# Second-stage attention scores: one float32 matmul replaced by three float32r passes over split q and k

## The chip, the cores and the metric

The kernel runs on one core of one Trainium2 chip. Its time is the device time of one execution in microseconds; the time before is the median of three runs. A separate, profiled execution gives the trace from which all durations below are read. PE is TensorE's matmul row, PEld its weight loads, DVE is VectorE, ACT is ScalarE, POOL is GpSimd, SP issues the DMAs.

## The reference

Two layers follow each other, with 8 batches of 576 tokens.

```python
# layer 1: 8 heads of width 64; heads 0-3 see the last 32 tokens, heads 4-7 every 32nd earlier token
scores = scale * np.matmul(q, k.transpose(0, 1, 3, 2))
scores = np.where(masks[None], scores, -1e9)
attn = softmax(scores);  x = np.matmul(attn, v)          # x: (8, 576, 512) after the heads are joined
# layer 2: 4 experts, each a causal attention of width 64 over x; the top 2 of 4 gate logits weigh them
logits = x @ w_gate
for e in range(4):
    q = x @ wq[e];  k = x @ wk[e];  v = x @ wv[e]
    scores = scale * (q @ k.transpose(0, 2, 1))
    scores = np.where(causal, -1e9, scores)
    a = softmax(scores)
    out += weight_of_e * (a @ v @ wo[e])
```

`wq` and `wk` are drawn eight times larger than the other weights, so the second layer's scores are wide and have to be computed with nearly full float32 precision.

## The kernel before, in words

Layer 1 is done per batch and pair of heads: `load_qk` brings q and k into a tile `nat`, `tp` (L514) transposes it on PE, `s` (L546) makes scores, `mask` and `softmax0` to `softmax5` run on DVE, POOL and ACT, `pt` (L604, L607) transposes the weights back, `xa` (L641, L658) multiplies with v. The result x is held as two float32r tiles, `xh` (rounded) and `xl` (the remainder).

Layer 2 is done per batch b and pair of experts ep (two pairs, so 16 rounds in all). `project` (L765, for the first batch L776) makes q and k of both experts of a pair at once: 128 rows, 64 for each expert, in two column halves of 288 tokens. Each half is twelve passes of 128 rows by 288 columns, three for each of the four slices of x (`xh` with the rounded weight, `xl` with the rounded weight, `xh` with the weight's remainder). `pj_out` copies each half from PSUM into the float32 tile `qk`, on ACT or DVE. `values2` (`vp`, L712) makes v and the gate logits the same way.

`attend` makes the scores. The 576 queries are four tiles of 128 and one of 64; tile t sees 128, 256, 384, 512 and 576 keys. For a 128-query tile (`s2`, L839) the two experts lie in rows 0 to 63 and 64 to 127 and are two float32 matmuls, each into a PSUM bank of its own. The last 64 queries (`s2_4`, L819) of both experts share one bank, expert 0 in partitions 0 to 63 and expert 1 in 64 to 127, in two key halves of 288. Then come `max2` and `max2_4` (DVE, L846, L825: scale, mask, row maximum), `exp2` (ACT, L851), `recip2` (DVE), `scale2` (POOL, L874), `t2` (L893, transposes on PE), `acc` (L926, times v), a split into `oh` and `ol`, and `yp` (L955, the output projection), whose result is stored.

PE knows four array shapes here: 128x128 (`pj`, `vp`, `yp`), row-split 64x128 (`tp`, `pt`, `s2`, `t2`), column-split 128x64 (`acc`, local `xa`) and 64x64 (`s`, `s2_4`, the other `xa`).

The order on each engine is written at build time. Every operation is registered with `op(kind, engines, key, ...)`, with an assumed duration for each engine that may take it, the buffers it reads and writes, and a key that is shifted by the table `PRI` (per kind, and per kind and batch). `schedule()` (L214) then walks through time and lets each engine take, among the operations that could start now, the one with the lowest key; buffers come from rings (`Ring`) of fixed size. What comes out is a fixed instruction stream for each engine: on the chip each engine runs its own in order, and a late operand holds up everything behind it. The rings that the change touches are `QK2` (the `qk` tiles, three), `TH` (transposed weights, four) and `PTR` (transposed layer-1 weights, two). While the kernel starts, the raw weights wq, wk and wv stand in the three `QK2` tiles, from where `hi_w` and `lo_w` split them.

Of the kernel before, what the change touches and what calls it, by code (L numbers as in the profile page):

```python
# [9 lines left out]
F32R = mybir.dt.float32r  # L10
# [10 lines left out]
def attention_moe_kernel(  # L21
# [59 lines left out]
    class Ring:  # L81
# [26 lines left out]
        "acc": 14.5, "acc 0": -193.0, "acc 1": 158.0, "acc 2": 1.0, "acc 3": 17.0, "acc 5": 37.5,  # L108
# [13 lines left out]
        "lo_w 0": -52.5, "load_qk": -6.0, "load_qk 0": -264.5, "load_qk 1": -15.0, "load_qk 2": -24.5,  # L122
        "load_qk 3": 76.0, "load_qk 4": 68.0, "load_qk 5": 107.5, "load_qk 6": 127.0, "load_qk 7": 164.0,
        "load_v": 6.0, "load_v 0": 5.5, "load_v 1": 5.5, "load_v 2": 30.0, "load_v 3": 36.0,
        "load_v 4": 15.5, "load_v 5": 55.5, "load_v 6": 96.5, "load_v 7": 74.5, "load_w": 9.0,
        "load_w 0": 21.0, "mask": 21.0, "mask 0": 137.5, "mask 1": -30.0, "mask 2": 124.0, "mask 3": 19.0,
# [248 lines left out]


    YS = ring("ys", [128, DM], 3)
    QK2 = ring("qk2", [128, 2, S], 3)
    W = {}

    def load_weights(name, key):
# [6 lines left out]
        for kt in range(nk):  # L388
# [3 lines left out]
            def raw(kt=kt, st=st):  # L392
                if wide:
                    return wide.t.rearrange("p a c -> p (a c)")[:, kt * n:kt * n + n]
# [636 lines left out]
```

## Time and profile before

| what | value |
|---|---|
| time, median of 3 runs | 492.1 us (491.94 to 493.04) |
| the profiled execution's own time | 494.44 us |
| its span, first to last instruction | 492.7 us |
| mean granted TensorE clock | 0.982 |
| PE busy | 473.5 us, 96% |
| DVE, ACT, POOL busy | 323.8, 293.8, 201.5 us |

Busy time of PE counts every matmul from its start to its modelled end, and these overlap; what a matmul costs the stream behind it is read from the distance between two starts in the timeline. A float32 matmul stands in the trace as two records (128 `s2` matmuls of the program are 256 records of L839), a float32r matmul as one. A group's tile name has its buffer number left out, and operands are given as partitions x columns.

### The profile page before, as it was taken

Reading aid. Unit: us, or ns where it says so; the run is one execution under the profiler, and the core shown is the slowest. Engines: PE = TensorE matmul, PEld = TensorE weight load, DVE = VectorE, ACT = ScalarE, POOL = GpSimd, SP = SyncE. Lnnn points to the kernel's source line nnn. Section 1 sums busy time; section 2 is a strip of 40 time slices with the busy share of each in tenths; the row PEclk is TensorE's granted clock in tenths of the full one; section 3 lists DMA queues with packets and bytes.
Section 4 is the critical chain, followed back from the end, with each engine's and each line's share of the span. In section 5 each row is a group of like instructions: output and inputs, shape, how many; then the busy total and the mean of one; then the engine's idle time right before and its main releaser. Section 6 shows DMA issues by size and latency. Waiting matters only on the chain.

```text
span 492.7 us, 17597 instructions
## 1 busy us (share of the span) xinstructions
PE 473.5 (96%) x7046; PEld 398.0 (81%) x7046; DVE 323.8 (66%) x1004; ACT 293.8 (60%) x838; POOL 201.5 (41%) x252
## 2 busy tenths in 40 slices
PE   7679999899999999999999999899999999999996
PEld 5569897789778888898778987688978897898774
DVE  5777778784689467775878646675577857616620
ACT  2557867564765368655786536565486647635642
POOL 5456655532365143451473424133236434501430
PEclk9877999999999999999999999999999999999999
DMA  7988942530156004730466101454043100200024
GB/s 144 175 156 185 172 109 70 115 73 25 36 167 171 1 2 115 183 65 2 100 178 165 56 0 48 142 130 87 25 108 120 38 0 24 93 25 1 1 85 129
DMA packets 88880, 43.35 MB, mean 88 GB/s; under 512 B 77024, under 2 KB 80480, under 8 KB 88800
## 3 DMA queue, kind: packets, MB, share of 16 engines
q1 hardware_dynamic: 88800, 42.24, 35.4%
q8 instruction: 56, 0.92, 0.8%
q14 instruction: 24, 0.20, 0.1%
HBM read 32.78 MB, written 9.44 MB: 86 GB/s over the span
## 4 chain that ended last, share of the span: by engine, by line
PE 90%; DMA 6%; SPq 2%; issue 1%; ACT 0%; ACTq 0%
PE bank L765 19%; PE bank L712 12%; PE bank L955 11%; PE bank L926 9%; PE bank L839 8%; PE bank L893 6%; DMA nat<-in_k_dram 6%; PE bank L514 5%; PE bank L546 4%; PE bank L641 4%; PE bank L819 4%; PE bank L776 3%; PE bank L658 3%; PE bank L604 2%; PE bank L607 1%; SPq L460 1%
## 5 line engine op out<-in xcount | busy, mean ns | idle before, releaser
L874 POOL TENSOR_SCALAR p<-p,st,wt 128x256 f32<-128x256 f32 (+3 forms) x128 | 75.8, 607 | 110.1 <-DVE st L858 44.7
L851 ACT ACTIVATE p<-p,st 128x128 f32<-128x128 f32 (+3 forms) x128 | 71.3, 560 | 10.8 <-DVE st L846 10.8
L846 DVE CUSTOM_DVE_ANT_0 p<-bank,m_cau 128x128 f32<-128x128 f32 (+3 forms) x128 | 56.6, 486 | 19.1 <-PE bank L839 17.2
L329 ACT COPY qk<-bank 128x288 f32<-128x288 f32 x48 | 19.2, 400 | 53.7 <-PE bank L765 50.4
L926 PE MATMUL bank<-th,vs 128*64 128x192 f32 (+4 forms) x512 | 50.5, 343 | 0.0
L329 ACT COPY th<-bank 128x256 f32<-128x256 f32 (+2 forms) x100 | 40.2, 428 | 13.0 <-PE bank L893 11.5
L329 ACT COPY qkt<-bank 128x324 f32<-128x324 f32 (+2 forms) x99 | 36.6, 424 | 18.4 <-PE bank L514 14.4
L572 POOL TENSOR_TENSOR p1l<-p1l,st 128x960 f32<-128x960 f32 (+1 forms) x18 | 29.1, 1626 | 42.7 <-DVE st L570 31.0
L926 PEld LDWEIGHTS bank<-th,vs 128*64 128x64 f32 x512 | 34.7, 138 | 14.1 <-issue 7.2
L712 PE MATMUL bank<-wh_v,xh 128*128 128x260 f32 (+1 forms) x160 | 46.0, 288 | 0.0
L712 PE MATMUL bank<-wh_v,xl 128*128 128x260 f32 (+1 forms) x160 | 45.3, 283 | 0.0
L712 PE MATMUL bank<-wl_v,xh 128*128 128x260 f32 (+1 forms) x160 | 45.2, 282 | 0.0
L893 PEld LDWEIGHTS bank<-ident,p 64*128 64x128 f32 x800 | 32.3, 139 | 15.3 <-issue 9.7
L839 PE MATMUL bank<-qk 64*128 64x128 f32 (+3 forms) x256 | 42.1, 449 | 0.0
L329 DVE COPY th<-bank 128x384 f32<-128x384 f32 (+2 forms) x60 | 29.1, 489 | 19.6 <-PE bank L893 17.4
L893 PE MATMUL bank<-ident,p 64*128 64x64 f32 x800 | 40.7, 230 | 0.0
L581 POOL TENSOR_TENSOR p1l<-p1l,st 128x960 f32<-128x960 f32 (+1 forms) x18 | 29.0, 1616 | 27.8 <-DVE st L579 24.3
L514 PE MATMUL bank<-ident,nat 54*128 54x54 f32 (+1 forms) x636 | 30.8, 233 | 8.5 <-DMA nat<-in_k_dram 7.2
L546 PE MATMUL bank<-qkt 64*64 64x54 f32 (+1 forms) x1408 | 35.0, 239 | 3.7 <-ACT qkt L329 1.6
L514 PEld LDWEIGHTS bank<-ident,nat 54*128 54x128 f32 (+1 forms) x636 | 25.8, 146 | 12.8 <-issue 7.5
L546 PEld LDWEIGHTS bank<-qkt 64*64 64x64 f32 x1408 | 29.8, 138 | 6.6 <-ACT qkt L329 3.2
L765 PE MATMUL bank<-xh,wh_k 128*128 128x288 f32 x112 | 33.8, 302 | 0.0
(138 smaller groups left out, 1241.3 us busy)
## 6 DMA issues: line engine op xcount, KB each, us to landing
out_dram<-ys SPq DMA_DIRECT2D x32, 256.0 KB
v<-in_v_dram SPq DMA_DIRECT2D x32, 192.0 KB
nat<-in_q_dram SPq DMA_DIRECT2D x28, 144.0 KB
nat<-in_k_dram SPq DMA_DIRECT2D x28, 144.0 KB
nat<-in_q_dram SPq DMA_DIRECT2D x32, 99.0 KB
nat<-in_k_dram SPq DMA_DIRECT2D x32, 99.0 KB
v<-in_v_dram SPq DMA_DIRECT2D x48, 54.0 KB
nat<-in_q_dram SPq DMA_DIRECT2D x16, 90.0 KB
```

Source lines behind the costliest of these rows:

```text
L329: (nc.scalar.copy if e == "ACT" else nc.vector.tensor_copy)(dst, src)
L514: nc.tensor.transpose(tp[x].t[:, w_ * (g - g0):w_ * (g - g0) + w_], blk, ident[r, r])
L546: nc.tensor.matmul(o, lhs, rhs, start=True, stop=True)
L712: nc.tensor.matmul(vp.t[:m, :NV], xx.t[:, t0:t0 + m], ww.t[:, kt, :], start=i == 0, stop=i == 11)
L765: nc.tensor.matmul(pj.t[:, :HS], ww.t[:, kt, ep * 128:(ep + 1) * 128], xx.t[:, c], start=i == 0, stop=i == 11)
L839: nc.tensor.matmul(sp[a].t[:, :nk], qk.t[r, 0, q0:q0 + 128], qk.t[r, 1, :nk], start=True, stop=True)
L846: lambda e, sp=sp, p=p, a=a, nk=nk, ci=ci: nc.vector.tensor_tensor_reduce(out=p.t[:, a, :nk], in0=sp[a].t[:, :nk], in1=m_cau[:, S - nk:], ...
L851: op("exp2", {"ACT": 0.485 + 0.00083 * nk}, k_ + 1, lambda e, p=p, a=a, ci=ci, nk=nk: nc.scalar.activation(p.t[:, a, :nk], p.t[:, a, :nk], ...
L874: lambda e, p=p, a=a, ci=ci, t=t, nk=nk: nc.gpsimd.tensor_scalar(p.t[:, a, :nk], p.t[:, a, :nk], st.t[:, 14 + ci + a:15 + ci + a], wt.t[:, ...
L893: nc.tensor.transpose(tp[hf].t[:, 64 * c:64 * c + 64], src, ident[r, r])
L926: nc.tensor.matmul(acc.t[o, c0:c0 + cn], vw, th[a].t[:, s0:s0 + cn], start=j == 0, stop=j == idx[-1], skip_group_check=True)
L955: nc.tensor.matmul(yp.t[:, :DM], xx.t[:, c0:c0 + 128], ww.t[:, ep, :], start=i == 0, stop=i == 5)
```

## The change

1. `pj_out` now always runs on ACT and writes `qk` rounded to float32r. A new operation `pj_lo` (DVE) subtracts this from the projection in PSUM and writes the remainder to a new tile `qkl` (float32r).
2. `s2` (L864 in the new file) is three float32r passes for each expert, accumulated in the same bank: q with k, q's remainder with k, q with k's remainder. The two experts' passes alternate.
3. For the last 64 queries a new operation `qd` (POOL, four copies of 64x64) lays q and its remainder of both experts on the diagonal of a 128x128 tile whose other half is zero. `s2_4` (L844) is then three full 128x128 passes of 288 columns instead of two float32 matmuls, and its array shape is that of the projections.
4. Buffers: `QK2` has two tiles instead of three, two `qkl` and two `qd` tiles are new, `PTR` has one instead of two. The raw weights wq and wk are staged in the `TH` tiles, wv in the tiles `P2[2]` of the weights of score tile 2.
5. Every entry of `PRI` has another value, and there are entries for `pj_lo` and `qd`.

```diff
     PRI = {
-        "acc": 14.5, "acc 0": -193.0, "acc 1": 158.0, "acc 2": 1.0, "acc 3": 17.0, "acc 5": 37.5,
+        "acc": 22.0, "acc 0": -338.0, "acc 1": 87.0, "acc 2": 51.5, "acc 3": 110.5, "acc 4": 29.0,
...
-    QK2 = ring("qk2", [128, 2, S], 3)
+    QK2 = ring("qk2", [128, 2, S], 2, F32R)
+    QKL = ring("qkl", [128, 2, S], 2, F32R)
+    QD = fixed("qd", [128, 2, 128], 2, F32R)
+    for t in QD.tiles:
+        for a in range(2):
+            nc.scalar.copy(t[64 * a:64 * a + 64, :, 64 - 64 * a:128 - 64 * a],
+                           m_cau[64 * a:64 * a + 64, :128].rearrange("p (i c) -> p i c", i=2))
...
-        wide = QK2.new(f"wst_{name}") if name != "o" else None
+        wide = [] if name == "o" else [(P2[2] if name == "v" else TH).new(f"wst_{name}{i}") for i in range(2)]
...
-    PTR = ring("pt1", [128, 2 * 2 * 5 * 64], 2)
+    PTR = ring("pt1", [128, 2 * 2 * 5 * 64], 1)
...
-            op("pj_out", either(HS), key + step * u + 0.5, lambda e, u=u, pj=pj: copy(
-                e, qk.t[:, j, u * HS:(u + 1) * HS], pj.t[:, :HS]), r=[pj], w=[qk[j, u]])
+            c_ = slice(u * HS, (u + 1) * HS)
+            op("pj_out", {"ACT": act(HS)}, key + step * u + 0.5, lambda e, c_=c_, pj=pj: nc.scalar.copy(
+                qk.t[:, j, c_], pj.t[:, :HS]), r=[pj], w=[qk[j, u]])
+            op("pj_lo", {"DVE": dve(HS)}, key + step * u + 0.8, lambda e, c_=c_, pj=pj: nc.vector.tensor_sub(
+                qk.lo.t[:, j, c_], pj.t[:, :HS], f(qk.t[:, j, c_])), r=[pj, qk[j, u]], w=[qk.lo[j, u]])
+        if j == 0:
+
+            def diag(e):
+                for i, x in enumerate((qk, qk.lo)):
+                    for a in range(2):
+                        r = slice(64 * a, 64 * a + 64)
+                        nc.gpsimd.tensor_copy(qk.d.t[r, i, r], f(x.t[r, 0, S - 64:]))
+
+            op("qd", {"POOL": 1.2}, key + step + 1, diag, r=[qk[0, 1], qk.lo[0, 1]], w=[qk.d])
...
-                        for a in range(2):
-                            r = slice(64 * a, 64 * a + 64)
-                            nc.tensor.matmul(sp.t[r, :HS], qk.t[r, 0, q0:q0 + 64], qk.t[r, 1, c0:c0 + HS],
-                                             start=True, stop=True)
+                        for i, (l, r) in enumerate(((0, qk), (1, qk), (0, qk.lo))):
+                            nc.tensor.matmul(sp.t[:, :HS], qk.d.t[:, l], r.t[:, 1, c0:c0 + HS], start=i == 0, stop=i == 2)
...
-                for a in range(2):
-                    r = slice(64 * a, 64 * a + 64)
-                    nc.tensor.matmul(sp[a].t[:, :nk], qk.t[r, 0, q0:q0 + 128], qk.t[r, 1, :nk], start=True, stop=True)
+                for i, (x, y) in enumerate(((qk, qk), (qk.lo, qk), (qk, qk.lo))):
+                    for a in range(2):
+                        r = slice(64 * a, 64 * a + 64)
+                        nc.tensor.matmul(sp[a].t[:, :nk], x.t[r, 0, q0:q0 + 128], y.t[r, 1, :nk], start=i == 0, stop=i == 2)
```

How this moves instructions is read from the built streams. First PE at the scores of the third batch, second pair of experts. Before, the last projection passes (L765) are followed by the four tiles of `s2` (L839), one matmul per expert and tile:

```order
L765 MATMUL bank6_70<-xl1_180,wh_q0_221 128x288
L765 MATMUL bank6_70<-xh1_174,wl_q0_222 128x288
L839 MATMUL bank1_65<-qk22_136 128x128
L839 MATMUL bank2_66<-qk22_136 128x128
L839 MATMUL bank4_68<-qk22_136 128x256
L839 MATMUL bank5_69<-qk22_136 128x256
L839 MATMUL bank7_71<-qk22_136 128x384
L839 MATMUL bank0_64<-qk22_136 128x384
L839 MATMUL bank3_67<-qk22_136 128x512
L839 MATMUL bank6_70<-qk22_136 128x512
```

The same place now (`qk2` is the rounded q and k, `qkl` the remainder; L779 is the projection, L864 the scores):

```order
L779 MATMUL bank2_66<-xl1_190,wh_q0_227 128x288
L779 MATMUL bank2_66<-xh1_184,wl_q0_228 128x288
L864 MATMUL bank4_68<-qk21_135 128x128
L864 MATMUL bank7_71<-qk21_135 128x128
L864 MATMUL bank4_68<-qk21_135,qkl1_137 128x128
L864 MATMUL bank7_71<-qk21_135,qkl1_137 128x128
L864 MATMUL bank4_68<-qkl1_137,qk21_135 128x128
L864 MATMUL bank7_71<-qkl1_137,qk21_135 128x128
L864 MATMUL bank1_65<-qk21_135 128x256
L864 MATMUL bank0_64<-qk21_135 128x256
```

A tile has three matmuls per expert where it had one, and the two experts' banks alternate. Here the twelve passes that fill bank2_66 (the last half of q) stand between the half that the first two tiles need and the first score pass. Counted over the whole PE stream, the array shape changes 259 times where it changed 249 times.

Second, ACT and DVE around the projections of the second batch's first pair of experts, in the new streams. On ACT, L799 is `pj_out`:

```order
L334 COPY ys0_131<-bank6_70 128x512
L799 CAST qk20_134<-bank2_66 128x288
L799 CAST qk20_134<-bank4_68 128x288
L334 COPY vs1_197<-bank3_67 128x260
L589 ACTIVATE p1s0_172<-p1s0_172 128x12x54
```

On DVE, L801 is `pj_lo`, L574 and L585 belong to layer 1's softmax:

```order
L574 TENSOR_TENSOR p1s1_175<-bank1_65,m_str_81 128x6x54
L801 TENSOR_TENSOR qkl0_136<-bank2_66,qk20_134 128x288
L585 TENSOR_REDUCE st12_181<-p1s0_172 128x12
L585 TENSOR_REDUCE st13_182<-p1s1_175 128x12
L801 TENSOR_TENSOR qkl0_136<-bank4_68,qk20_134 128x288
```

All 64 copies of projected q and k stand on ACT now (48 stood there and 16 on DVE), and DVE has 64 subtractions more, each behind its copy and in line with layer 1's reductions. Third, POOL for the same pair of experts, where L809 is `qd`, L596 the last softmax step of layer 1 and L899 is `scale2`:

```order
L596 TENSOR_TENSOR p1s1_175<-p1s1_175,st13_182 128x12x54
L809 CAST qd0_138<-qk20_134 64x64 x2
L809 CAST qd0_138<-qkl0_136 64x64 x2
L899 TENSOR_SCALAR p200_144<-p200_144,st24_209,wt1_204 128x128 x2
```

The four copies are new on POOL (64 in the whole program). The last-queries matmuls (`s2_4`) stand on PE as three passes in each of the two key halves. On SP the loads while the kernel starts stand in nearly the same order: half of wk has moved from behind the loads of the second batch's third pair of heads (L467 before, L482 now) to ahead of them.

More of the change, by code (lines that the diff above doesn't have):

```diff
@@ L107, in attention_moe_kernel @@
     PRI = {
-        "acc": 14.5, "acc 0": -193.0, "acc 1": 158.0, "acc 2": 1.0, "acc 3": 17.0, "acc 5": 37.5,
[13 rows of a table removed]
[L122 to L126, printed above, removed]
[54 rows of a table removed]
+        "acc": 22.0, "acc 0": -338.0, "acc 1": 87.0, "acc 2": 51.5, "acc 3": 110.5, "acc 4": 29.0,
[13 rows of a table added]
+        "hi_w 0": -109.0, "lo_w": -136.0, "lo_w 0": -81.0, "load_qk": -71.5, "load_qk 0": -231.5,
+        "load_qk 1": 42.5, "load_qk 2": 62.5, "load_qk 3": 62.5, "load_qk 4": 48.5, "load_qk 5": 53.0,
+        "load_qk 6": 118.5, "load_qk 7": 126.5, "load_v": 64.0, "load_v 0": -64.5, "load_v 1": -53.5,
+        "load_v 2": -5.5, "load_v 3": 12.5, "load_v 4": 103.5, "load_v 5": 85.5, "load_v 6": 60.5,
+        "load_v 7": 56.0, "load_w": 1.0, "load_w 0": 12.5, "mask": -142.0, "mask 0": 196.5, "mask 1": -43.0,
[10 rows of a table added]
+        "pj_lo 6": -117.5, "pj_lo 7": 197.0, "pj_out": -189.5, "pj_out 0": -8.5, "pj_out 1": 326.5,
[38 rows of a table added]
+        "vp_out": -284.5, "vp_out 0": 186.0, "vp_out 1": 209.0, "vp_out 2": -203.0, "vp_out 3": 60.5,
+        "vp_out 4": 242.0, "vp_out 5": 1.0, "vp_out 6": 18.0, "vp_out 7": 18.5, "warm": 148.5,
[6 rows of a table added]
+        "yp_out": -38.0, "yp_out 0": -354.0, "yp_out 1": 56.5, "yp_out 2": 74.5, "yp_out 3": 88.5,
+        "yp_out 4": -22.5, "yp_out 5": 103.5, "yp_out 6": -149.0, "yp_out 7": 44.0,
     }
@@ L377, in attention_moe_kernel @@
     YS = ring("ys", [128, DM], 3)
-    QK2 = ring("qk2", [128, 2, S], 3)
+    QK2 = ring("qk2", [128, 2, S], 2, F32R)
[5 more added lines that the diff above has]
+                           m_cau[64 * a:64 * a + 64, :128].rearrange("p (i c) -> p i c", i=2))
     W = {}
+    P2 = [ring(f"p2{t}", [128, 2, S if t == 3 else q0 + m], 2) for t, (q0, m) in enumerate(QT[:4])]
+    P2.append(fixed("p24", [128, S + 64], 2, value=lambda t: [t[:, S:]]))
+    TH = ring("th", [128, 832], 4)
     def load_weights(name, key):
@@ L386, in load_weights @@
         W[name] = (hi, lo)
-        wide = QK2.new(f"wst_{name}") if name != "o" else None
+        wide = [] if name == "o" else [(P2[2] if name == "v" else TH).new(f"wst_{name}{i}") for i in range(2)]
         for kt in range(nk):
-            st = wide[kt] if wide else YS.new(f"wst_{name}{kt}")
+            st = wide[kt // 2][kt % 2] if wide else YS.new(f"wst_{name}{kt}")
             k_ = key + 0.1 * kt
@@ L393, in raw @@
                 if wide:
-                    return wide.t.rearrange("p a c -> p (a c)")[:, kt * n:kt * n + n]
+                    t = wide[kt // 2].t
+                    t = t.rearrange("p a c -> p (a c)") if name == "v" else t
+                    return t[:, kt % 2 * n:kt % 2 * n + n]
                 return st.t
@@ L414, in load_weights @@
                r=[st, hi[kt]], w=[lo[kt]])
-    P2 = [ring(f"p2{t}", [128, 2, S if t == 3 else q0 + m], 2) for t, (q0, m) in enumerate(QT[:4])]
-    P2.append(fixed("p24", [128, S + 64], 2, value=lambda t: [t[:, S:]]))
     NAT = fixed("nat", [128, (11 * 2 + 1) * D], 2, value=lambda t: [t[:, c * D:(c + 1) * D] for c in (10, 21, 22)])
@@ L683, in attention_moe_kernel @@
     ST2 = ring("st2", [128, 24], 6)
-    TH = ring("th", [128, 832], 4)
     OHR = ring("oh", [128, DM], 3, F32R)
@@ L816, in mml @@
                     def mml(e, sp=sp, c0=c0, q0=q0):
-                        for a in range(2):
-                            r = slice(64 * a, 64 * a + 64)
-                            nc.tensor.matmul(sp.t[r, :HS], qk.t[r, 0, q0:q0 + 64], qk.t[r, 1, c0:c0 + HS],
-                                             start=True, stop=True)
-                    op("s2_4", {"PE": HS * 4 / 2400 + 0.02}, k_ + 0.2 * hh, mml, r=[qk[0, 1], qk[1, hh]],
-                       w=[sp, p[0]], mode=MQ)
+                        for i, (l, r) in enumerate(((0, qk), (1, qk), (0, qk.lo))):
+                            nc.tensor.matmul(sp.t[:, :HS], qk.d.t[:, l], r.t[:, 1, c0:c0 + HS], start=i == 0, stop=i == 2)
+                    op("s2_4", {"PE": HS * 3 / 2400 + 0.04}, k_ + 0.2 * hh, mml, r=[qk.d, qk[1, hh], qk.lo[1, hh]],
+                       w=[sp, p[0]], mode=M128)
                     op("max2_4", {"DVE": 0.23 + 0.00102 * HS}, k_ + 0.5 + 0.2 * hh,
@@ L836, in mm @@
             def mm(e, sp=sp, q0=q0, nk=nk):
-                for a in range(2):
-                    r = slice(64 * a, 64 * a + 64)
-                    nc.tensor.matmul(sp[a].t[:, :nk], qk.t[r, 0, q0:q0 + 128], qk.t[r, 1, :nk], start=True, stop=True)
-            op("s2", {"PE": nk * 4 / 2400 + 0.02}, k_, mm,
-               r=[qk[0, u] for u in us] + [qk[1, u] for u in range((nk - 1) // HS + 1)],
+                for i, (x, y) in enumerate(((qk, qk), (qk.lo, qk), (qk, qk.lo))):
+                    for a in range(2):
+                        r = slice(64 * a, 64 * a + 64)
+                        nc.tensor.matmul(sp[a].t[:, :nk], x.t[r, 0, q0:q0 + 128], y.t[r, 1, :nk], start=i == 0, stop=i == 2)
+            op("s2", {"PE": nk * 3 / 2400 + 0.03}, k_, mm,
+               r=[x[0, u] for u in us for x in (qk, qk.lo)] + [x[1, u] for u in range((nk - 1) // HS + 1) for x in (qk, qk.lo)],
                w=[*sp, p[0], p[1]], mode=MR)
@@ L988, in attention_moe_kernel @@
         qk = [QK2.new(f"qk_{b}_{ep}") for ep in range(2)]
+        for ep in range(2):
+            qk[ep].lo, qk[ep].d = QKL.new(f"qkl_{b}_{ep}"), QD.new(f"qd_{b}_{ep}")
         project(b, 0, qk[0], "k", k2, 2.5)
```

134 rows, old and new, of the table PRI are left out of this document.

## The prediction

> **What bounds the kernel now.** I read the page first: the busy shares, the slices and the chain that ended last.
>
> ```profile
> span 492.7 us, 17597 instructions
> ...
> PE 473.5 (96%) x7046; PEld 398.0 (81%) x7046; DVE 323.8 (66%) x1004; ACT 293.8 (60%) x838; POOL 201.5 (41%) x252
> ...
> PE   7679999899999999999999999899999999999996
> ...
> PEclk9877999999999999999999999999999999999999
> ...
> PE 90%; DMA 6%; SPq 2%; issue 1%; ACT 0%; ACTq 0%
> ```
>
> PE is busy in nearly every slice and carries 90% of the chain; DMA's 6% lie mostly in the first slices, where the granted clock is also below full. A busy share can hide a latency chain, so I split the span and looked for idle time on PE.
>
> ```profile
> 0.00:36.26 36.26, 25.32 (x516) 21.23 (x517) 24.47 (x70) 15.66 (x39) 18.96 (x36) 0.89 0.88 158
> 36.26:480.00 443.74, 440.04 (x6477) 370.63 (x6477) 298.40 (x931) 274.50 (x791) 182.55 (x216) 0.99 0.32 81
> ```
>
> ```profile
> 36.26 1.50 PE L514 MATMUL bank<-ident,nat 54*128 54x54 f32 x23 [2.75 <-DMA nat<-in_k_dram]
> ...
> 91.62 0.33 PE L546 MATMUL bank<-qkt 64*64 64x54 f32 x5 [1.29 <-issue]
> ...
> 317.70 0.55 PE L514 MATMUL bank<-ident,nat 54*128 54x54 f32 x11 [2.18 <-DMA nat<-in_k_dram]
> ```
>
> The two rows of the first are stretches: start and end, length, then busy time of PE, PEld, DVE, ACT and POOL, then clock, DMA share and GB/s. Up to 36.26 us PE idles for 10.9 us and the last thing it waits for is a load: the start is set by loads at 158 GB/s. From there to 480 us PE idles for 3.7 of 443.7 us, almost all in the last two rows of the second, which are from the timeline of PE (start, length, work, and in brackets the idle time before it and what ended it). None of them is a wait for the copied q and k. So from 36 us on the time is the sum of what PE streams, and a matmul that takes less of the stream shortens the kernel, as long as nothing makes PE wait. All score matmuls of layer 2 come after 50 us, in this part.
>
> **What a pass costs the stream.** The mean durations of the groups overlap each other, so I take distances between starts.
>
> ```profile
> 212.23 0.28 PE L712 MATMUL bank<-wh_v,xh 128*128 128x260 f32 x1
> ...
> 213.68 0.30 PE L765 MATMUL bank<-xh,wh_k 128*128 128x288 f32 x1
> ...
> 216.69 0.30 PE L765 MATMUL bank<-xh,wh_q 128*128 128x288 f32 x1
> ...
> 218.29 0.29 PE L712 MATMUL bank<-wh_v,xh 128*128 128x260 f32 x1
> ...
> 247.97 0.40 PE L955 MATMUL bank<-wh_o,ol 128*128 128x512 f32 x1
> ...
> 248.90 0.39 PE L955 MATMUL bank<-wl_o,oh 128*128 128x512 f32 x1
> ```
>
> Twelve float32r passes of 260 columns lie between the first two starts: 1.45/12 = 0.121 us each. Twelve of 288 lie between the next two: 1.60/12 = 0.133. Four of 512 lie between the last two: 0.93/4 = 0.2325. That is a line of 0.0056 us + 0.443 ns a column. Now the float32 scores:
>
> ```profile
> 219.62 0.28 PE L712 MATMUL bank<-wl_v,xh 128*128 128x260 f32 x1
> 219.83 0.52 PEld L839 LDWEIGHTS bank<-qk 64*128 64x128 f32 x8
> 219.83 0.93 PE L839 MATMUL bank<-qk 64*128 64x128 f32 x8
> 219.94 0.38 ACT L329 COPY vs<-bank 128x260 f32<-128x260 f32 x1 [0.40 <-PE bank L712]
> ...
> 220.59 0.22 PE L604 MATMUL bank<-ident,p1l 64*96 64x64 f32 x2
> ...
> 224.47 1.77 PE L839 MATMUL bank<-qk 64*128 64x384 f32 x8
> ...
> 226.17 0.34 PE L712 MATMUL bank<-wh_v,xh 128*64 128x260 f32 x1
> ...
> 246.12 1.19 PE L819 MATMUL bank<-qk 64*64 64x288 f32 x8
> 247.24 0.46 PE L893 MATMUL bank<-ident,p 64*128 64x64 f32 x8
> ```
>
> Tiles of 128 and 256 keys, both experts, take 0.76 us (219.83 to 220.59); those of 384 and 512 take 1.70 (224.47 to 226.17). The second pair has 512 columns more and is followed by another array shape, which costs about 0.09 (219.62 to 219.83 is 0.21, a pass is 0.12). So 512 columns more cost 0.85 us, 1.66 ns a column for both experts together: four times the slope of a float32r pass, with the experts side by side. A round has 1280 columns, 2.125 us without lead and hand-over. The two matmul pairs of the last queries take 1.12 us (246.12 to 247.24).
>
> **The change part by part.** *Scores of the full tiles.* New: three passes per tile, experts side by side. The weights bring a floor:
>
> ```profile
> L712 PEld LDWEIGHTS bank<-wh_v,xl 128*128 128x128 f32 x128 | 24.1, 189 | 0.0
> ...
> L712 PEld LDWEIGHTS bank<-wh_v,xl 128*64 128x64 f32 x32 | 4.3, 134 | 0.0
> ```
>
> A load of 128 columns lasts 55 ns more than one of 64, so its rate is 0.11 us for 128 columns, whatever latency lies in the rest. A pass of 128 keys streams less than that (0.062 by the line) and pays the load. So 3 x (0.110 + 0.119 + 0.176 + 0.2325) = 1.91 us a round by the float32r line. With the slope of the row-split matmuls and no constant (0.415 ns a column, again with 0.110 as the least) it is 3 x (0.110 + 0.110 + 0.159 + 0.2125) = 1.77. Against 2.125 the 16 rounds give back 3.4 to 5.6 us. No float32r pass in a row-split shape is in the trace; the type speaks for the first, the shape for the second, and I take the middle, **4.5 us**.
>
> *Scores of the last queries.* Two times three passes of 288 are 6 x 0.133 = 0.80 us; with a first load of 0.11 and a change of shape of 0.09, 1.00 against 1.12: 1.9 us over 16 rounds. Without lead and change on both sides it is 0.956 (2 x 288 x 1.66 ns) against 0.80: 2.5 us. I take **2.3 us**.
>
> *Array shapes.* 259 changes instead of 249, at about 0.09: **minus 0.9 us**.
>
> *The remainder and the diagonal* are new work beside PE, with these rows:
>
> ```profile
> L628 DVE TENSOR_TENSOR xl<-bank,xh 128x320 fp32r<-128x320 f32 x16 | 7.7, 481 | 1.9 <-ACT xh L626 1.8
> ...
> L628 DVE TENSOR_TENSOR xl<-bank,xh 128x256 fp32r<-128x256 f32 x16 | 6.6, 414 | 0.3 <-ACT xh L626 0.2
> ...
> L329 ACT COPY qk<-bank 128x288 f32<-128x288 f32 x48 | 19.2, 400 | 53.7 <-PE bank L765 50.4 <-PE bank L776 3.3
> ...
> L329 DVE COPY qk<-bank 128x288 f32<-128x288 f32 x16 | 7.3, 457 | 16.3 <-PE bank L765 14.4 <-POOL p L874 1.9
> ...
> L752 POOL COPY wt<-wt 64x2 f32<-64x2 f32 x8 | 1.4, 178 | 39.1 <-DVE wt L743 39.1
> ...
> L874 POOL TENSOR_SCALAR p<-p,st,wt 128x128 f32<-128x128 f32 x32 | 14.0, 447 | 104.6 <-DVE st L858 39.7 <-DVE wt L743 23.2 <-ACT p L851 13.3
> ```
>
> DVE gains 64 subtractions of 288 columns at 0.447 (between 414 and 481 ns), 28.6 us, and loses 16 copies, 7.3: 345 us at most, 71% of the span. ACT gains 16 x 0.400 = 6.4 us, 300 in all. A 64x64 copy on POOL is not in the trace; it lies between the 64x2 copy (0.18) and the 128x128 multiplication (0.45), so 64 of them are 11 to 29 us, at most 230 in all. No engine comes near PE. What counts is latency: scores now wait for ACT's copy and then DVE's subtraction. The matmul's end lies some 0.17 us after its last column (0.29 long, 0.12 apart), so the copy, the subtraction and three hand-overs of 0.04 (`vp`'s last pass ends at 219.90, ACT's copy of it starts at 219.94) need 0.17 + 0.40 + 0.45 + 0.12 = 1.14 us; before, one copy needed about 0.7. I counted the PE work that stands between the projection half a tile needs last and its first score pass, at the rates above. Before, the least distance was 0.75 us, and PE still did not idle there. In the new stream it is 1.60 us (twelve projection passes are 1.60), and for the last queries, which also wait for four POOL copies (0.7 to 1.8 us), 3.5 us. Both are more than needed, by 0.4 us at the tightest place, so I cost the new waits at nothing; the cover is other PE work already placed there. Without it each of the 32 groups of score tiles would pay 0.45 to 2 us.
>
> *Start and buffers.* While the kernel starts, 256 KB of wk now stand ahead of the load PE waits for last, 1.6 us at 158 GB/s; in PE's new order some 2.2 us more projection work stands ahead of that wait too. I take nothing for this, with 2 us either way. One `pt1` and two `qk` tiles less narrow what may run ahead; the 3.5 us of waits left between 36 and 480 us can vanish or double, again counted as nothing.
>
> **Sum.** 4.5 + 2.3 - 0.9 = 5.9 us. The profiled execution took 494.4 us, 1.8 around its span, so it would take 488.5. It is 2.3 us above the median of the runs, 492.1; the saving is the same there: **486.2 us**. With all PE terms at their ends the saving is 4.4 to 7.2; with start and waits 2 to 3 us either way the forecast's own range is 482.5 to 489.5.
>
> **The rivals.** *Weights cannot be loaded under a pass of the same rows.* Then each of the twelve passes of a round pays its 0.110 in the open: 1.59 (3 x 1280 x 0.415 ns) + 1.32 = 2.91 us against 2.125, 12.6 us more over 16 rounds, and with the other terms the result is 492.1 + 12.6 - 1.4 = 503 us, slower. It would decide as soon as more than a third of the loads lie open. Against it: the eight loads at 219.83 are over after 0.52 us while the matmuls stream to 220.59, and projection passes, each with its own 128-column load into all rows, follow each other every 0.133 us, where 0.110 in the open would make 0.23. For it: the row-split shape has now 24 loads in a round where it had 16, never measured at one pass each. Chance 0.05. The Trainium skill has such a rule in "TensorE: Matmul & The Clock Gate", Part 3 on packing small matmuls, The mechanism: weight loads overlap with matmuls in flight only where the row group differs. This trace disagrees with it in the 0.133 us of the projections.
>
> *The new latency chain stalls PE.* DVE stands in a row of layer-1 reductions of up to 1.15 us, POOL in ones of 1.8:
>
> ```profile
> L576 DVE TENSOR_REDUCE st<-p1l 128x10 f32<-128x960 f32 x14 | 16.1, 1147 | 2.3 <-ACT p1l L574 2.2
> ...
> L572 POOL TENSOR_TENSOR p1l<-p1l,st 128x960 f32<-128x960 f32 x14 | 25.3, 1808 | 38.7 <-DVE st L570 27.0 <-DVE st L578 8.0 <-PE bank L514 3.7
> ```
>
> One that starts just ahead of a subtraction makes it 0.8 us late where the distance is 1.6 to 2.3 us. Some eleven places are that close: up to 8 us, which eats the gain, 491 to 494. Against it: before, with 0.75 us of distance, none of these waits came. Chance 0.11, half of it above 492.
>
> *More is gained*: the waits of 3.5 us vanish and the loads of the narrow tiles hide better (0.06 instead of 0.11 for 128 keys, 2.4 us): 478 to 482.5. Chance 0.15.
>
> *The three passes are not cheaper*: a float32r pass in the row-split shape costs what a float32 matmul does. Then 3 x 2.125 a round, 68 us more, about 559. All float32r passes of the trace run at a quarter of the float32 slope. Chance 0.02.
>
> **How the numbers follow.** The forecast has 0.67, the others 0.05, 0.11, 0.15 and 0.02. The range 480.5 to 491.0 holds the forecast's own, most of what is gained more and the milder stalls, about 0.82. A measurement of this kernel tells 0.2% from no change, 1 us: faster means below 491.1. That is 0.67 + 0.15 + some 0.05 of the stalls, 0.87; the same 0.04, slower 0.09.
>
> **What would show it.** Score rows of full tiles: 384 float32r records, starts of one round adding up to 1.77 to 1.91 us, loads under passes. The last queries: 96 records, 0.133 apart. PE's idle time after the start still about 3.5 us and none of it before scores; DVE near 340 us. The prediction is wrong if PE waits before scores for more than 3 us in all, if the narrow tiles' passes lie further apart than 0.11, or if the start takes more than 2 us longer.

## The result, and the profile after

The changed kernel takes 484.58 us (median of 4 runs, 483.85 to 485.07) where the kernel before, in the same comparison, takes 492.02 (491.74 to 493.04). The ratio is 0.984 with a 95% interval of 0.981 to 0.987: faster by 7.4 us. The forecast was 486.2 in a range of 480.5 to 491.0.

The page of the changed kernel's profiled execution (485.07 us), with the rows that answer to those shown of before:

```profile
span 483.3 us, 17865 instructions
...
PE 467.7 (97%) x7142; PEld 409.1 (85%) x7142; DVE 343.4 (71%) x1041; ACT 304.3 (63%) x868; POOL 216.9 (45%) x317
...
PE   7698999999999999999999999999999999999996
...
PEclk9679999999999999999999999999999999999998
...
PE 92%; DMA 4%; SPq 1%; ACT 1%; issue 1%; DVE 1%; ACTq 0%; DVEq 0%
```

PE is still the bound: 92% of the chain that ended last, with 5.8 us less busy time although it issues 96 matmuls more. DVE gained 19.6 us and POOL 15.4, and neither comes near.

Next its busy times by stretches (start and end, length, then PE, PEld, DVE, ACT, POOL, clock, DMA share, GB/s), and the longest waits of PE (what waits, for what: us in total, times, longest):

```profile
0.00:36.26 36.26, 28.57 (x515) 24.08 (x518) 22.86 (x65) 17.27 (x45) 18.16 (x35) 0.81 0.87 156
36.26:470.60 434.34, 431.04 (x6596) 378.88 (x6589) 320.08 (x975) 283.66 (x816) 198.75 (x283) 1.00 0.33 84
```

```profile
PE bank L529 <- DMA nat<-in_k_dram: 2.2, 1, 2.2
PE bank L790 <- DVE xl L643: 1.8, 1, 1.8
PE bank L1000 <- DVE p1l L342: 1.2, 1, 1.2
...
PE bank L918 <- ACT pt L334: 0.5, 1, 0.5
```

From 36.26 to 470.60 us PE idles for 434.34 - 431.04 = 3.3 us, as before (3.7). The last wait for a load in the start was 2.75 us before and is 2.2 now. No score matmul (L844, L864) is among the waits, here or in the rows left out: the new chain of copy, subtraction and diagonal copy never holds PE up.

The stream itself, in the timeline of the changed kernel (start, length, work): a wide tile, the last queries, and a pair of narrow tiles with weight loads (PEld) beside it.

```profile
165.59 0.48 PE L864 MATMUL bank<-qk 64*128 64x512 f32 x2
165.83 0.47 PE L864 MATMUL bank<-qk,qkl 64*128 64x512 f32 x2
166.05 0.48 PE L864 MATMUL bank<-qkl,qk 64*128 64x512 f32 x2
...
168.64 0.54 PE L844 MATMUL bank<-qk,qd 128*128 128x288 f32 x2
169.01 0.29 PE L844 MATMUL bank<-qkl,qd 128*128 128x288 f32 x1
...
169.54 0.29 PE L779 MATMUL bank<-xh,wh_k 128*128 128x288 f32 x1
...
218.22 0.19 PEld L864 LDWEIGHTS bank<-qk 64*128 64x128 f32 x2 [0.16 <-issue]
218.22 0.33 PE L864 MATMUL bank<-qk 64*128 64x128 f32 x2
218.33 0.19 PEld L864 LDWEIGHTS bank<-qk,qkl 64*128 64x128 f32 x2
...
218.39 0.27 PE L864 MATMUL bank<-qk,qkl 64*128 64x128 f32 x2
218.44 0.19 PEld L864 LDWEIGHTS bank<-qkl,qk 64*128 64x128 f32 x2
218.50 0.27 PE L864 MATMUL bank<-qkl,qk 64*128 64x128 f32 x2
218.55 0.19 PEld L864 LDWEIGHTS bank<-qk 64*128 64x128 f32 x2
218.61 0.34 PE L864 MATMUL bank<-qk 64*128 64x256 f32 x2
218.66 0.19 PEld L864 LDWEIGHTS bank<-qk,qkl 64*128 64x128 f32 x2
218.78 0.28 PE L864 MATMUL bank<-qk,qkl 64*128 64x256 f32 x2
218.78 0.19 PEld L864 LDWEIGHTS bank<-qkl,qk 64*128 64x128 f32 x2
...
218.90 0.28 PE L864 MATMUL bank<-qkl,qk 64*128 64x256 f32 x2
```

"x2" are the two experts side by side. A pass of 512 keys takes 0.24 and 0.22 us to the next start. The last queries take 0.90 us (168.64 to 169.54) where they took 1.12. The loads of 0.19 us lie under the passes. The narrow tiles show what the forecast did not have: from the second pass to the third it is 0.11 and 0.12 us, but the first of each tile takes 0.17. Over the whole trace the median distance from the second pass to the third is 0.112, 0.117, 0.175 and 0.233 us for 128 to 512 keys, 0.64 together. That is what the forecast's float32r line gave (0.6375), not the slope of the row-split matmuls (0.59). The groups of one shape each (busy us, mean ns of one, idle before) show longer first passes over all 16 rounds:

```profile
L864 PE MATMUL bank<-qk 64*128 64x512 f32 x32 | 6.6, 398 | 0.0
L864 PE MATMUL bank<-qkl,qk 64*128 64x512 f32 x32 | 6.5, 392 | 0.0
...
L864 PE MATMUL bank<-qk 64*128 64x384 f32 x32 | 6.3, 385 | 0.0
L864 PE MATMUL bank<-qkl,qk 64*128 64x384 f32 x32 | 5.5, 334 | 0.0
...
L864 PE MATMUL bank<-qk 64*128 64x256 f32 x32 | 5.4, 332 | 0.0
L864 PE MATMUL bank<-qk 64*128 64x128 f32 x32 | 5.2, 320 | 0.0
...
L864 PE MATMUL bank<-qkl,qk 64*128 64x256 f32 x32 | 4.5, 277 | 0.0
L864 PE MATMUL bank<-qkl,qk 64*128 64x128 f32 x32 | 4.4, 272 | 0.0
```

First passes are longer by 48, 55, 51 and 6 ns (128 to 512 keys): 0.16 us a round. These means mix two cases, and what stands ahead of the tile tells them apart. Behind work other than scores the first pass takes 0.164 us for 128 keys and 0.27 for 384 (medians). Behind the next narrower score tile it takes 0.170 for 256 keys, 0.05 more than a later pass, but 0.175 for 384 and 0.231 for 512, no more than a later one. The loads suggest why. In the narrow pair they start 0.11 to 0.12 us apart (218.22 to 218.78), the time that the forecast gave to a load. The first of them has no score pass to lie under, and the load for the first pass of 256 keys starts at 218.55, only 0.06 us ahead of that pass. This is read from the starts; no run tells it from a price of the change of shape.

By tile, both experts, the mean stream of the two kernels is 0.31 us before and 0.39 now for 128 keys, 0.46 and 0.44 for 256, 0.69 and 0.57 for 384, 0.92 and 0.785 for 512. The narrowest tile became dearer, and the gain comes from the two widest.

To see where time went, I gave every matmul of a trace the distance from its start to the next one's start, less PE's idle time between, and added these up by kind of work. A second profile of each kernel shows what one execution adds (us):

| | before | before, again | after | after, again |
|---|---|---|---|---|
| full tiles (`s2`) | 38.1 | 38.2 | 35.1 | 35.1 |
| last queries (`s2_4`) | 17.6 | 17.8 | 15.0 | 15.0 |
| all else that PE streams | 417.4 | 415.3 | 417.2 | 417.0 |
| PE idle up to 37 us | 9.7 | 8.2 | 6.4 | 6.9 |
| PE idle later | 3.7 | 3.7 | 3.3 | 2.7 |

The score rows are steady to 0.2 us. They give 3.1 and 2.7 us. The shorter idle time at the start gives 1.3 to 3.3 more. The rest of the stream differs by up to 2.1 us between two executions of one kernel, so what it contributes is not settled by these traces.

### The profile page after: what moved, and what is told of

It reads as the page before. It is cut to its first block, busy times and chain, and to the rows that moved or that the text cites. A ratio compares the mean times of both kernels' runs of the same rounds, so it can differ in the third digit from the quotient of the medians.

```text
span 483.3 us, 17865 instructions
## 1 busy us (share of the span) xinstructions
PE 467.7 (97%) x7142; PEld 409.1 (85%) x7142; DVE 343.4 (71%) x1041; ACT 304.3 (63%) x868; POOL 216.9 (45%) x317
## 4 chain that ended last, share of the span: by engine, by line
PE 92%; DMA 4%; SPq 1%; ACT 1%; issue 1%; DVE 1%; ACTq 0%; DVEq 0%
PE bank L779 19%; PE bank L726 12%; PE bank L980 12%; PE bank L951 10%; PE bank L864 7%; PE bank L918 7%; PE bank L561 6%; PE bank L529 5%; PE bank L656 4%; PE bank L844 3%; DMA nat<-in_k_dram 3%; PE bank L673 3%; PE bank L619 2%; PE bank L790 2%; PE bank L622 1%; SPq L475 1%
## 5 line engine op out<-in xcount | busy, mean ns | idle before, releaser
L899 POOL TENSOR_SCALAR p<-p,st,wt 128x128 f32<-128x128 f32 (+3 forms) x128 | 76.1, 608 | 107.2 <-DVE st L883 62.3
L799 ACT CAST qk<-bank 128x288 fp32r<-128x288 f32 x64 | 25.5, 399 | 55.6 <-PE bank L779 50.0
L334 ACT COPY qkt<-bank 128x324 f32<-128x324 f32 (+2 forms) x109 | 40.7, 429 | 15.0 <-PE bank L529 14.3
L334 ACT COPY th<-bank 128x384 f32<-128x384 f32 (+2 forms) x98 | 39.4, 435 | 14.5 <-PE bank L918 12.0
L801 DVE TENSOR_TENSOR qkl<-bank,qk 128x288 fp32r<-128x288 f32 x64 | 28.2, 451 | 18.8 <-ACT qk L799 18.4
L334 DVE COPY th<-bank 128x256 f32<-128x256 f32 (+2 forms) x62 | 29.0, 479 | 14.3 <-PE bank L918 12.5
L596 POOL TENSOR_TENSOR p1l<-p1l,st 128x960 f32<-128x960 f32 (+1 forms) x18 | 29.2, 1625 | 21.7 <-DVE st L594 19.5
L561 PE MATMUL bank<-qkt 64*64 64x54 f32 (+1 forms) x1408 | 33.8, 240 | 1.5 <-ACT qkt L334 0.6
L779 PE MATMUL bank<-xh,wh_k 128*128 128x288 f32 x112 | 33.6, 300 | 0.0
L779 PE MATMUL bank<-xh,wh_q 128*128 128x288 f32 x112 | 33.2, 296 | 0.0
L779 PE MATMUL bank<-xh,wl_k 128*128 128x288 f32 x112 | 33.0, 295 | 0.0
```

What stands on the lines that cost most here:

```text
L334: (nc.scalar.copy if e == "ACT" else nc.vector.tensor_copy)(dst, src)
L561: nc.tensor.matmul(o, lhs, rhs, start=True, stop=True)
L779: nc.tensor.matmul(pj.t[:, :HS], ww.t[:, kt, ep * 128:(ep + 1) * 128], xx.t[:, c], start=i == 0, stop=i == 11)
L899: lambda e, p=p, a=a, ci=ci, t=t, nk=nk: nc.gpsimd.tensor_scalar(p.t[:, a, :nk], p.t[:, a, :nk], st.t[:, 14 + ci + a:15 + ci + a], wt.t[:, ...
```

## The experiments

The theory: the gain is what the forecast said, two cheaper score forms on a PE-bound stream, with side work that is covered. The rivals: the gain comes from the new order and buffers; the copy and subtraction cost something after all; the passes gain only by alternating between experts, or lose by loads.

**Undoing one score form at a time.** All else stays as in the changed kernel, its order table included.

```diff
# full tiles as float32 (s2_f32)
-                for i, (x, y) in enumerate(((qk, qk), (qk.lo, qk), (qk, qk.lo))):
-                    for a in range(2):
-                        r = slice(64 * a, 64 * a + 64)
-                        nc.tensor.matmul(sp[a].t[:, :nk], x.t[r, 0, q0:q0 + 128], y.t[r, 1, :nk], start=i == 0, stop=i == 2)
+                for a in range(2):
+                    r = slice(64 * a, 64 * a + 64)
+                    nc.tensor.matmul(sp[a].t[:, :nk], f(qk.t[r, 0, q0:q0 + 128]), f(qk.t[r, 1, :nk]), start=True, stop=True)
# last queries as two float32 matmuls (s24_f32)
-                        for i, (l, r) in enumerate(((0, qk), (1, qk), (0, qk.lo))):
-                            nc.tensor.matmul(sp.t[:, :HS], qk.d.t[:, l], r.t[:, 1, c0:c0 + HS], start=i == 0, stop=i == 2)
+                        for a in range(2):
+                            r = slice(64 * a, 64 * a + 64)
+                            nc.tensor.matmul(sp.t[r, :HS], f(qk.t[r, 0, q0:q0 + 64]), f(qk.t[r, 1, c0:c0 + HS]),
+                                             start=True, stop=True)
```

> The changed kernel with the full score tiles back in float32 form (one float32 matmul per expert, on the rounded q and k; the remainders are left out of these tiles), every instruction stream otherwise in the order of the changed kernel. If the time is what PE streams (the forecast's step), the full tiles' starts go from 35.1 back to 38.1 us and the time rises by 3.1 us, to 487.7 (487 to 489). If the gain came from the re-set order and fewer waits, the time stays within 1 us of 484.6.

> The changed kernel with the last queries' scores back in float32 form (two 64x64 float32 matmuls in each key half, on the rounded q and k without remainders), order otherwise as in the changed kernel; the diagonal tile is still made. Forecast's step: 17.6 instead of 15.0 us of PE stream, so 2.7 us more, 487.3, and up to 1 us on top, since a 64x64 shape now stands where its neighbours have another. If it was the order: within 1 us of 484.6.

> Both score forms back to float32 in the changed kernel's order, with the subtractions and diagonal copies still done. Forecast's step: the two add up, 5.8 us more, 490.4; what is left to the 492.0 of the kernel before, 1.6 us, is then the order and the waits. If the order carried the gain: 485 to 486.

Beside these the kernel before was profiled once more.

> The kernel before, profiled once more. Its first profiled execution took 494.4 us, 2.3 above its median, with one wait of 2.18 us for a load at 316 us. If that wait belongs to this one execution, it is gone or short here and the span is near 490.3; if it belongs to the order of the loads, it is there again with about 2 us.

| kernel | median us (range, runs) | ratio to before (95%) | `s2` stream | `s2_4` stream |
|---|---|---|---|---|
| before, beside these | 491.6 (489.7 to 495.9, 29) | 1 | 38.2 | 17.8 |
| full tiles float32 | 490.3 (488.0 to 492.8, 12) | 0.9975 (0.9952 to 0.9999) | 38.8 | 15.0 |
| last queries float32 | 489.7 (488.0 to 492.0, 12) | 0.9961 (0.9940 to 0.9982) | 35.1 | 18.0 |
| both float32 | 493.2 (490.8 to 495.7, 12) | 1.0024 (0.9997 to 1.0051) | 38.8 | 18.0 |

With both undone the gain is gone: 1.0024 against 0.984, 8.7 us by the medians. So the score forms carry it, and all the rest of the change together (order, buffers, side work) costs about 0.2%, at the edge of what can be told from nothing. All three times lie above what was expected of them (at most 489, 488.3 and 490.4). Undone alone, the full tiles are worth 5.7 us and the last queries 5.1; the changed kernel did not run beside them here. The sum of the two is 10.8, more than 8.7, and their streams differ by only 3.7 and 3.0 us. Both the halves and the sum are thus larger in time than in the score rows.

Part of that is scatter: the profiled execution with the full tiles in float32 was the shortest of its twelve (488.03), and against the profiled one of the changed kernel, the longest of its four (485.07), it takes 3.0 us more. In the profiled executions PE's whole busy time rises from 467.7 us to 471.1 (full tiles), 471.4 (last queries) and 476.7 (both). With both undone 6.7 of these 9.0 us are score rows; the other 2.2 are work of PE that the edit does not touch, and neither edit alone shows them. Why that work streams longer there is not shown.

In the second profile of before, PE's wait of 2.18 us at 317.70 is shorter and has another releaser (timeline of PE, start, length, work, idle before and what ended it):

```profile
316.13 0.55 PE L514 MATMUL bank<-ident,nat 54*128 54x54 f32 x11 [1.16 <-DVE p1l L559]
```

About half of that wait belonged to the one execution, though the total after 37 us came out at 3.7 again.

**The side work taken away.** With both forms in float32 nothing reads the remainder or the diagonal tiles, so they can go without a race; the outputs stay those of the float32 scores.

```diff
-            op("pj_lo", {"DVE": dve(HS)}, key + step * u + 0.8, lambda e, c_=c_, pj=pj: nc.vector.tensor_sub(
-                qk.lo.t[:, j, c_], pj.t[:, :HS], f(qk.t[:, j, c_])), r=[pj, qk[j, u]], w=[qk.lo[j, u]])
+            op("pj_lo", {"DVE": dve(HS)}, key + step * u + 0.8, lambda e: None, r=[pj, qk[j, u]], w=[qk.lo[j, u]])
...
-                        nc.gpsimd.tensor_copy(qk.d.t[r, i, r], f(x.t[r, 0, S - 64:]))
+                        pass
```

> The changed kernel with both score forms back in float32 and, beyond that, without the 64 subtractions and the 64 diagonal copies, which nothing reads any more; order otherwise the same. What is left of the change is its order, its buffers and the rounding. With float32 scores but the subtractions and copies kept, the ratio was 1.0024. If the side work of DVE and POOL is covered, as the forecast has it, the ratio stays within 0.002 of that; if the side work cost the missing 1 to 2 us, it falls to 0.998 to 1.000.

> The changed kernel again, next to the kernel before on the chip that also runs the version below. The ratio should be 0.984 as first measured (0.981 to 0.987); if the single-edit runs with float32 scores were dearer only because their chip was another, this one is dearer too, at 0.987 or above.

Without the side work: 493.0 us (491.4 to 495.8, 12 runs), ratio 1.0036 (1.0015 to 1.0058), no faster than with it (1.0024). Its busy row on the page shows that DVE and POOL are indeed relieved, by 24.1 and 15.4 us against the same kernel with the side work (343.7 and 217.6):

```profile
PE 476.7 (97%) x7046; PEld 397.5 (81%) x7046; DVE 319.6 (65%) x977; ACT 304.2 (62%) x868; POOL 202.2 (41%) x253
```

Costing it at nothing was right: with float32 scores the work itself costs nothing, and in the changed kernel no score matmul waits for it. The changed kernel itself, run again on this chip, took 484.2 us (483.6 to 484.9, 6 runs), ratio 0.9854 (0.9828 to 0.9880). On one chip, then, the kernel with both forms undone is 8.8 us slower.

**How far the cover reaches.** Each `pj_lo` does its subtraction two or three times, which makes the remainder 0.45 or 0.90 us later.

```diff
# lo_x2; lo_x3 has range(3)
-            op("pj_lo", {"DVE": dve(HS)}, key + step * u + 0.8, lambda e, c_=c_, pj=pj: nc.vector.tensor_sub(
-                qk.lo.t[:, j, c_], pj.t[:, :HS], f(qk.t[:, j, c_])), r=[pj, qk[j, u]], w=[qk.lo[j, u]])
+            op("pj_lo", {"DVE": dve(HS)}, key + step * u + 0.8, lambda e, c_=c_, pj=pj: [nc.vector.tensor_sub(
+                qk.lo.t[:, j, c_], pj.t[:, :HS], f(qk.t[:, j, c_])) for _ in range(2)], r=[pj, qk[j, u]], w=[qk.lo[j, u]])
```

> Every subtraction that makes a remainder is done twice (the second repeats the first), same order: DVE busy 28 us more (372 us, 77%) and each remainder 0.45 us later. The forecast put 0.4 us of cover at the tightest place: the time rises by 0 to 1 us, to at most 485.6, with PE's idle time up by less than 1 us. If the new chain was on the path, each of 32 groups of score tiles pays: 5 us or more.

> Every subtraction done three times: DVE busy 56 us more (400 us, 82%) and each remainder 0.9 us later. With cover of 0.4 us at the tightest places and about eleven places within 0.8 us of them, 11 x up to 0.5 us: 2 to 6 us more, 486.5 to 490.5, as idle time of PE before score tiles. If DVE alone had room and no score tile waits: below 485.6.

Twice: 487.0 us (484.8 to 487.5, 4 runs), 0.9881 (0.9827 to 0.9935), 2.4 more than the changed kernel by the medians and above the 485.6 expected, though the intervals overlap; PE's idle time after 37 us did not rise (3.0 against 3.3). Three times: 502.9 (499.7 to 504.5), 1.0205 (1.0142 to 1.0268), 18.3 more, where 2 to 6 were expected. The waits of PE, first with two subtractions, then with three:

```profile
PE bank L864 <- DVE qkl L801: 0.3, 1, 0.3
```

```profile
PE bank L864 <- DVE qkl L801: 8.6, 14, 1.8
PE bank L529 <- DMA nat<-in_k_dram: 3.0, 2, 2.3
...
PE bank L779 <- DVE qkl L801: 0.9, 1, 0.9
```

The count of tight places was about right, the cover somewhat too large: with 0.45 us more one score tile waits, for 0.3 us, so the cover there is nearer 0.15 than 0.4; with 0.90 more fourteen wait, where some eleven were counted. These waits make up 8.6 us of the 18.3, PE idles for 13.0 us after 37 us in all, and the stream itself grows by 7.8 (475.1 against 467.3), 4.5 of it in the score tiles. That would fit waits too short to outlast the end of the matmul before, which do not show as idle time. The price of 0.45 to 2 us for a group without cover holds for the longest wait (1.8) but says nothing of the work that is pushed back behind it.

**One pass less, and another order of the passes.** The first leaves out the third pass of the full tiles, rounded q times the remainder of k, so it computes less; the second does all three passes of one expert ahead of the other's.

```diff
# two_pass
-                for i, (x, y) in enumerate(((qk, qk), (qk.lo, qk), (qk, qk.lo))):
+                for i, (x, y) in enumerate(((qk, qk), (qk.lo, qk))):
...
-                        nc.tensor.matmul(sp[a].t[:, :nk], x.t[r, 0, q0:q0 + 128], y.t[r, 1, :nk], start=i == 0, stop=i == 2)
+                        nc.tensor.matmul(sp[a].t[:, :nk], x.t[r, 0, q0:q0 + 128], y.t[r, 1, :nk], start=i == 0, stop=i == 1)
# no_alt
-                for i, (x, y) in enumerate(((qk, qk), (qk.lo, qk), (qk, qk.lo))):
-                    for a in range(2):
+                for a in range(2):
+                    for i, (x, y) in enumerate(((qk, qk), (qk.lo, qk), (qk, qk.lo))):
```

> The changed kernel without the third pass (q with k's remainder) in the full score tiles, same order. Forecast's step: a pass of 128, 256, 384 and 512 keys costs the stream 0.128, 0.144, 0.176 and 0.233 us by the distances in the changed kernel's trace, 0.68 a round, so 16 rounds give 10.9 us back: 473.7 (472.5 to 475.5). If another engine or a chain of waits has become the bound, less than half of it comes back.

> The changed kernel with the experts' passes of a full tile not alternating: three passes of the first expert, then three of the second, same order otherwise. If the halves run side by side only where they stand next to each other in the program, five pass times instead of three are paid per tile: 0.68 x 2 = 1.36 us a round, 22 us, 506. If PE pairs them anyway, as the two-record float32 matmuls of the kernel before were paired: 484.6.

Two passes: 478.6 us (477.5 to 478.9, 4 runs), 0.9715 (0.9666 to 0.9765), 6.0 less than the changed kernel, where 10.9 less were expected. The `s2` stream falls by 9.3 us (35.1 to 25.8), 0.58 a round, by tile 0.112, 0.118, 0.163 and 0.186. For the narrow tiles that is what a later pass takes, so the expectation's 0.128 and 0.144 were too high. For 512 keys it is 0.05 less than a pass (0.233): the work behind the last pass starts later, 0.36 us after it in the mean where it was 0.32. Three passes at 0.6375 are 1.91 us a round, and a round's stream is 2.19 (35.1/16): 0.28 us lie in lead, hand-over and the longer first passes. Before, the same remainder was 0.26 (38.1/16 - 2.125). The timeline of this kernel, the pair of narrow tiles up to the first start after it:

```profile
217.24 0.33 PE L864 MATMUL bank<-qk 64*128 64x128 f32 x2
217.41 0.27 PE L864 MATMUL bank<-qk,qkl 64*128 64x128 f32 x2
217.52 0.33 PE L864 MATMUL bank<-qk 64*128 64x256 f32 x2
217.69 0.28 PE L864 MATMUL bank<-qk,qkl 64*128 64x256 f32 x2
217.90 0.39 PE L726 MATMUL bank<-wh_v,xh 128*128 128x260 f32 x1
```

The first pass of each of these tiles still takes 0.17 us, so this does not depend on the number of passes. Of the 9.3 us, 7.0 reach the span (476.3 against 483.3): PE idles 1.3 us more and streams 1.2 us more elsewhere.

Passes that do not alternate: 485.3 us (484.7 to 486.0, 4 runs), 0.9852 (0.9794 to 0.9910), the same as alternating. The trace shows why (timeline):

```profile
219.05 0.34 PE L864 MATMUL bank<-qk 64*128 64x128 f32 x2
219.16 0.20 PEld L864 LDWEIGHTS bank<-qk,qkl 64*128 64x128 f32 x2
219.22 0.28 PE L864 MATMUL bank<-qk,qkl 64*128 64x128 f32 x2
...
219.33 0.28 PE L864 MATMUL bank<-qkl,qk 64*128 64x128 f32 x2
```

PE still starts the passes in pairs, although its instruction stream has three of one expert ahead of the other's first.

**The order table by itself.** The changed kernel with the `PRI` of before, and the kernel before with the changed one's `PRI` (the whole table exchanged, nothing else, and every order made anew from it).

> The changed kernel with the table of shifts of the kernel before (none for the two new kinds of work), so that the whole order is made anew. Forecast's step: PE streams the same work, 467.3 us plus shape changes, and only waits differ; with waits as in the other two kernels 484 to 489. If the new shifts carried the gain: 490 or more.

> The kernel before with the table of shifts of the changed kernel. Forecast's step: the stream of PE is that of the kernel before, so 490 to 496, depending on waits. If the new shifts carried the gain: 485 to 488.

The changed kernel in the old order: 504.8 us (504.2 to 505.2, 4 runs), 1.0270 (1.0219 to 1.0322). The kernel before in the new order: 500.7 (499.3 to 501.1, 4 runs), 1.0191 (1.0130 to 1.0251). Busy rows and waits of PE of the first:

```profile
PE 479.5 (95%) x7142; PEld 419.0 (83%) x7142; DVE 339.8 (68%) x1044; ACT 304.4 (61%) x863; POOL 217.8 (43%) x319
```

```profile
PE bank L524 <- DMA nat<-in_k_dram: 6.2, 6, 1.7
PE bank L524 <- DMA nat<-in_q_dram: 2.6, 3, 1.2
```

Its stream is 479.1 us (467.3 in its own order), PE idles 9.0 us after 37 us (3.3), and PE changes its array shape 277 times (259). So my expectation that the old table would cost only a few us fails, and so does the one for the kernel before (490 to 496). Nor does the new table make the gain: on the old work it costs 8.6 to 10.4 us. Each table serves its own work, and the new shifts are needed to collect what the score forms save.

## Why the prediction was right, and where its terms were off

- **What bounds it.** Right: PE idles 3.3 us between 36 and 470 us, and undoing the two forms gives the whole gain back. That the sum comes so near is partly luck: the two score terms, 6.8 us, came to 5.8, and the rest of the 7.4 comes from terms that were costed at nothing or taken off.
- **Full tiles, 4.5 us (3.4 to 5.6).** The mis-sized term: 3.1 by the stream, below its lower end. Of the two rates that the forecast averaged, the type decided and not the shape: later passes take 0.112, 0.117, 0.175 and 0.233 us, the float32r line with its floor of 0.110, which gives 3.4 us. What is around the passes was taken as unchanged and grew from 0.26 to 0.28 us a round, 0.4 us; the longer first passes are 0.16 us a round of what lies there now. The sign named as speaking against the prediction, narrow passes further apart than 0.11, did come: 0.112 and 0.117 for later passes, but 0.164 and 0.170 for first ones, 0.13 and 0.15 in the mean of all.
- **Last queries, 2.3 us (1.9 to 2.5).** 2.7 by the stream, above its upper end. The 96 passes lie 0.133 apart in the median, as forecast.
- **Array shapes, 0.9 us lost.** Counted in the traces as in the built streams, 259 changes against 249, ten as forecast. Their cost lies inside the rows above and the rest of the stream and was not measured alone.
- **Remainder and diagonal, nothing.** Right: no wait before scores, and taking the work away gains nothing. DVE came to 343.4 us (345 at most forecast), ACT to 304.3 (300), and the POOL copy, bounded by 0.18 and 0.45 us, takes 0.232 (groups of the changed kernel):

```profile
L809 POOL CAST qd<-qk 64x64 fp32r<-64x64 f32 x32 | 7.4, 232 | 13.6 <-ACT qk L799 12.7
```

- **Start and buffers, nothing, 2 us either way.** The start's idle time is 1.3 to 3.3 us shorter, later waits up to 1.0. This makes up for the full tiles, so the forecast of 5.9 us met 7.4 partly by terms that offset each other. With both forms in float32 the start idles as little (5.9 us) and the kernel is not faster than before, so a shorter start is not a gain of its own. There the rest of PE's stream is 2 to 4 us longer than in the two profiles of before; whether that is the price of the new order was not isolated.
- **The rivals.** Loads in the open (503) and passes at float32's price (559) fall with the rows at 218 us: passes 0.11 and 0.12 apart with 0.19 us loads under them. The Trainium skill's rule in "TensorE: Matmul & The Clock Gate", Part 3, The mechanism, that loads overlap with matmuls in flight only where the row group differs, does not hold for these passes either: with each load of 0.11 in the open, the 256-key passes would stand near 0.23 us apart, and 0.117 is measured. (The same section also has PE pull a load ahead when it goes to a background weight buffer, and that these rows do not contradict.) A stalling chain (491 to 494) fails with the empty list of waits before scores; with two more subtractions in each `pj_lo` it is real. More gained (478 to 482.5) did not come: the 128-key passes lie 0.112 apart, a load's time, where this rival needed 0.06.

## What to carry to other kernels

Price a matmul form on a PE-bound kernel by the distances between starts, tile by tile, and price the first pass of a group by itself: the narrowest tile became dearer here (0.31 to 0.39 us) while the two widest won. Side work on an engine that is far from full costs nothing while its latency fits the PE work that stands ahead of it, so work out that distance: here 0.45 us more cost some 2 us and 0.90 more cost 18. A hand-tuned order belongs to the work it was tuned for (9 to 20 us with the other's), so undo parts of a change inside one order, and never judge it in the old one.

## What the runs showed that I had not expected

- PE pairs the matmuls of the two row halves by itself: with six passes written as three and three, starts stay together and the time is the same (485.3 and 484.6 us). What stands ahead of the prediction, that each engine runs its stream in order, is thus not exact for the starts of matmuls on different row halves.
- The first float32r pass of a score tile takes 0.05 us more than its successors for 128 and for 256 keys and 0.1 more for 384 behind other work, but nothing more for 384 and 512 keys behind another score tile.
- Kernels whose score forms are float32, in whole or in part, scatter more from execution to execution: 488.0 to 492.8, 488.0 to 492.0, 490.8 to 495.7 and 491.4 to 495.8 us over 12 runs each, and the kernel before 489.7 to 495.9 over 29, against 483.6 to 485.1 for the changed kernel over 10. But the two kernels with more subtractions, float32r throughout, scatter as much in four runs (484.8 to 487.5 and 499.7 to 504.5), so the score form is not the whole of it. Two profiles of before differ by 1.8 us in the stream and 1.5 in the start. What causes it stays open.
- Undone one by one, the two forms are worth 10.8 us, together 8.7. In the profiled executions PE's busy time says the reverse, 3.4 and 3.7 one by one and 9.0 together, so the surplus of the single edits is not in those traces. Whether it is scatter was not settled.
